# A depthwise convolution on four 64x64 tiles of the TensorE array in place of sixteen 32x32 tiles

## Chip, cores, metric

One core of one Trainium2 chip. The metric is device time in microseconds (us) of one execution; medians of several executions are quoted. Ratios compare fast runs alone: a run more than 1.5% above the fastest of its kernel counts as slow. (Single runs of a one-core program have no state of their own and are marked.)

## The reference

Pooled attention, then a gated feed-forward layer, for 8 batches of 576 tokens. What matters here is the second half, in which the gate is a depthwise convolution of three taps along the tokens:

```python
h = np.maximum(x @ w_in, 0.0)                 # x: 8 x 576 x 512, h: 8 x 576 x 1024
for k in range(3):
    conv_out += conv_w[k] * hp[:, k:k + S, :] # hp: h padded by one token on both sides
gate = 1.0 / (1.0 + np.exp(-conv_out))
return (h * gate) @ w_out
```

## The kernel before

The channels of h lie on the partitions, 8 blocks (`fb`) of 128, tokens along the free dimension. `mm1` makes one block of h, with the relu on ScalarE. `conv` is done by TensorE: three taps, each a product with a diagonal matrix, accumulated in PSUM. A 128x128 diagonal matrix wastes nearly all of the array, so the kernel uses 32x32 tiles: quarter `r` of block `j` goes through the tile in row `r` and column `(r + j) % 4`. All 16 tiles then work at once on four blocks, but block `j` comes out turned by `j` quarters. `gate` multiplies tanh of it with h, partition by partition, so it needs h turned in the same way; SBUF-to-SBUF copies make that turned h. Shortened:

```python
def h_row(b, fb):
    g, j = divmod(fb, NQ)                                  # NQ = 4, QD = 32
    return hT[b % 2][:, g, j + NQ - 1 if j else 0, :]

def mm1(b, fb):                                            # (products into ps cut)
    nc.scalar.activation(out=row..., in_=ps[:, :, 0:SC], func=ACT.Relu, scale=0.5)
    g, j = divmod(fb, NQ)
    if j:
        turned = hT[b % 2][:, g, j, :]
        cut = P - QD * j
        nc.sync.dma_start(out=turned[P - cut:P, PAD:S + PAD], in_=row[0:cut, PAD:S + PAD])
        nc.sync.dma_start(out=turned[0:P - cut, PAD:S + PAD], in_=row[cut:P, PAD:S + PAD])

def conv(b, g, c2):                                        # 4 blocks, half of the tokens
    ps = [slot("c_ps") for _ in range(2)]
    for kk in range(KW):
        for j in range(NQ):
            for r in range(NQ):
                c = (r + j) % NQ
                nc.tensor.matmul(out=ps[j // 2][QD * c:QD * (c + 1), j % 2, 0:SC],
                                 lhsT=dw[QD * r:QD * (r + 1), kk, g * NQ + j, :],
                                 rhs=row[QD * r:QD * (r + 1), o0:o0 + SC], ...)
    for i in range(2):
        nc.scalar.activation(out=tg[:, 2 * i:2 * i + 2, :], in_=ps[i][:, :, 0:SC], func=ACT.Tanh)

def gate(b, g, c2):                                        # VectorE: (tanh + 1) * turned h
    nc.vector.tensor_scalar(out=t1, in0=tg, scalar1=1.0, scalar2=None, op0=OP.add)
    nc.vector.tensor_tensor(out=gT..., in0=t1, in1=hT[b % 2][:, g, 0:NQ, ...], op=OP.mult)
```

PSUM is cut into four slots of two banks, and every product takes the next slot in turn, so TensorE can be held up until ScalarE or VectorE has emptied an old one. The instruction order is fixed by hand: the attention of batch b+1 is woven into the feed-forward layer of batch b.

The softmax here doesn't subtract the row's maximum and nothing guards it: scores larger than these inputs give would overflow.

Of the kernel before, what the change touches and what calls it, by code (L numbers as in the profile page):

```python
# [9 lines left out]
FP32 = mybir.dt.float32  # L10
BF16 = mybir.dt.bfloat16
AX = mybir.AxisListType
OP = mybir.AluOpType
ACT = mybir.ActivationFunctionType

@with_exitstack
def kernel(
# [10 lines left out]
    nc = tc.nc  # L28

    B, H, S, D = q.shape  # L30
# [3 lines left out]
    P = 128  # L34
# [4 lines left out]
    SC = 288  # L39
    NS = S // SC  # L40
# [2 lines left out]
    n_dmc = d_model // P  # L43
    n_fb = d_ff // P
    KW = 3
    QD = 32
    NQ = P // QD
    n_grp = n_fb // NQ
    PAD = 2
    tok0 = [0, 128, 256, 384, S - P]  # L50

    const_pool = ctx.enter_context(tc.tile_pool(name="const", bufs=1))
# [13 lines left out]
    def slot(name):  # L66
        return psum.tile([P, 2, BANK], FP32, name=name, tag="slot")

    def slot16(name):
        return psum.tile([P, 2, 2 * BANK], BF16, name=name, tag="slot")  # L70

    ident = const_pool.tile([P, P], BF16)
# [4 lines left out]
    w_out_sb = const_pool.tile([P, n_fb, d_model], BF16)  # L77
    cw_rows = const_pool.tile([KW * n_fb, P], FP32)
    convw = const_pool.tile([P, KW * n_fb], FP32)
    tile_id = const_pool.tile([P, QD], FP32)  # L80
    dw = const_pool.tile([P, KW, n_fb, QD], BF16)
    kz = [const_pool.tile([P, H, 2, Sp], BF16, name=f"kz{i}") for i in range(2)]
    va = [const_pool.tile([Sp, H, D + 1], BF16, name=f"va{i}") for i in range(2)]
    hT = [
        const_pool.tile([P, n_grp, 2 * NQ - 1, S + 2 * PAD], BF16, name=f"hT{i}") for i in range(2)
    ]

    def h_row(b, fb):
        g, j = divmod(fb, NQ)
        return hT[b % 2][:, g, j + NQ - 1 if j else 0, :]  # L90

    kv_view = "h (sp p) d -> sp h p d"
    q_view = "h (g r) d -> (h g) (r d)"
# [3 lines left out]
    def load_k(b, h0, n):  # L97
        if h0 == 0:
            st[b] = {"k": kv_pool.tile([Sp, H, POOL, D], BF16, name="kr")}
        nc.gpsimd.dma_start(  # L100
            out=st[b]["k"][:, h0:h0 + n], in_=k[b, h0:h0 + n].rearrange(kv_view, p=POOL)
        )
# [8 lines left out]
    def load_q(b):  # L111
        st[b]["q"] = q_pool.tile([P, NI, 2 * D], BF16, name="qr")
        nc.gpsimd.dma_start(  # L113
            out=st[b]["q"].rearrange("p i x -> p (i x)"), in_=q[b].rearrange(q_view, g=QG)
        )

    def landed(ap):
        nc.gpsimd.tensor_copy(out=seen, in_=ap)
# [114 lines left out]
    def mm1(b, fb):  # L233
        xT = st[b]["xT"]
        ps = slot("h_ps")
        for c in range(NS):
            for dc in range(n_dmc):
                nc.tensor.matmul(  # L238
                    out=ps[:, c, 0:SC],
                    lhsT=w_in_sb[:, dc, fb * P:(fb + 1) * P],  # L240
                    rhs=xT[:, dc, c * SC:(c + 1) * SC],
                    start=(dc == 0),
                    stop=(dc == n_dmc - 1),
                )
        row = h_row(b, fb)
        nc.scalar.activation(  # L246
            out=row[:, PAD:S + PAD].rearrange("p (c n) -> p c n", c=NS),
            in_=ps[:, :, 0:SC],
            func=ACT.Relu,
            scale=0.5,  # L250
        )
        g, j = divmod(fb, NQ)
        if j:
            turned = hT[b % 2][:, g, j, :]
            cut = P - QD * j
            nc.sync.dma_start(out=turned[P - cut:P, PAD:S + PAD], in_=row[0:cut, PAD:S + PAD])
            nc.sync.dma_start(out=turned[0:P - cut, PAD:S + PAD], in_=row[cut:P, PAD:S + PAD])

    def conv(b, g, c2):
        if "gT" not in st[b]:  # L260
            st[b]["gT"] = (
                st[b - 1]["gT"] if b % 2 else gT_pool.tile([P, n_fb, 2 * S], BF16, name="gT")
            )
        gT = st[b]["gT"]
        ps = [slot("c_ps") for _ in range(2)]
        for kk in range(KW):
            o0 = PAD - 1 + c2 * SC + kk
            for j in range(NQ):
                row = h_row(b, g * NQ + j)
                for r in range(NQ):  # L270
                    c = (r + j) % NQ
                    nc.tensor.matmul(  # L272
                        out=ps[j // 2][QD * c:QD * (c + 1), j % 2, 0:SC],
                        lhsT=dw[QD * r:QD * (r + 1), kk, g * NQ + j, :],
                        rhs=row[QD * r:QD * (r + 1), o0:o0 + SC],
                        start=(kk == 0),
                        stop=(kk == KW - 1),
                    )
        tg = tg_pool.tile([P, NQ, SC], BF16, name="tg")
        for i in range(2):  # L280
            nc.scalar.activation(  # L281
                out=tg[:, 2 * i:2 * i + 2, :], in_=ps[i][:, :, 0:SC], func=ACT.Tanh
            )
        st[b]["tg", g, c2] = tg

    def gate(b, g, c2):
        tg = st[b].pop(("tg", g, c2))
        t1 = tg_pool.tile([P, NQ, SC], BF16, name="tg1")
        nc.vector.tensor_scalar(out=t1, in0=tg, scalar1=1.0, scalar2=None, op0=OP.add)
        g0 = (b % 2) * S + c2 * SC  # L290
        nc.vector.tensor_tensor(  # L291
            out=st[b]["gT"][:, g * NQ:(g + 1) * NQ, g0:g0 + SC],
            in0=t1,
            in1=hT[b % 2][:, g, 0:NQ, PAD + c2 * SC:PAD + (c2 + 1) * SC],
            op=OP.mult,
        )

# [19 lines left out]
    def load_w_in(i, n):  # L317
        w = d_ff // n
        nc.gpsimd.dma_start(
            out=w_in_sb[:, :, i * w:(i + 1) * w],  # L320
            in_=moe_w_in.rearrange("(c p) f -> p c f", p=P)[:, :, i * w:(i + 1) * w],
        )

    def load_w_out(j):
        src = moe_w_out.rearrange("(g j p) m -> j p g m", j=NQ, p=P)
        dst = w_out_sb.rearrange("p (g j) m -> j p g m", j=NQ)
        cut = P - QD * j
        nc.gpsimd.dma_start(out=dst[j, P - cut:P], in_=src[j, 0:cut])
        if j:
            nc.gpsimd.dma_start(out=dst[j, 0:P - cut], in_=src[j, cut:P])  # L330

    def build_conv_w():
        ps = slot("cw_ps")
        nc.tensor.transpose(
            out=ps[:, 0, 0:KW * n_fb], in_=cw_rows, identity=ident32[0:KW * n_fb, 0:KW * n_fb]
        )
        nc.vector.tensor_copy(out=convw, in_=ps[:, 0, 0:KW * n_fb])
        for r in range(NQ):
            nc.vector.tensor_copy(
                out=tile_id[QD * r:QD * (r + 1), :],  # L340
                in_=ident[QD * r:QD * (r + 1), QD * r:QD * (r + 1)],
            )
        nc.vector.tensor_tensor(
            out=dw.rearrange("p k f j -> p (k f) j"),
            in0=tile_id.unsqueeze(1).to_broadcast([P, KW * n_fb, QD]),
            in1=convw.unsqueeze(2).to_broadcast([P, KW * n_fb, QD]),
            op=OP.mult,
        )

# [8 lines left out]
    def start():  # L358
        nc.sync.dma_start(out=cw_rows, in_=moe_conv_w.rearrange("k (fb p) -> (k fb) p", p=P))
        st[0] = {}  # L360
        load_k(0, 0, HH)
        load_q(0)
        make_identity(nc, ident)
        make_identity(nc, ident32)
        load_k(0, HH, HH)
        for i in range(2):
            nc.vector.memset(kz[i], 0.0)
            nc.vector.memset(va[i][:, :, D], float(POOL))
            nc.gpsimd.memset(hT[i][:, :, :, 0:PAD], 0.0)
            nc.gpsimd.memset(hT[i][:, :, :, S + PAD:S + 2 * PAD], 0.0)  # L370
        landed(st[0]["k"][0:1, 0, 0, 0:1])
        load_v(0, 0, HH)
        landed(st[0]["q"][0:1, 0, 0:1])
        load_v(0, HH, HH)
        landed(st[0]["k"][0:1, HH, 0, 0:1])
        load_w_in(0, 4)
        landed(st[0]["v"][0:1, 0, 0, 0:1])
        load_w_in(1, 4)
        landed(st[0]["v"][0:1, HH, 0, 0:1])
        load_w_in(2, 4)  # L380
        load_w_in(3, 4)
        landed(w_in_sb[0:1, 0, d_ff // 4:d_ff // 4 + 1])
        load_k(1, 0, H)
        landed(w_in_sb[0:1, 0, d_ff - 1:d_ff])
        load_q(1)
        landed(st[1]["k"][0:1, 0, 0, 0:1])
        load_v(1, 0, H)
        landed(st[1]["q"][0:1, 0, 0:1])
        for j in range(NQ):
            load_w_out(j)  # L390
        build_conv_w()
        build_perm()
        k_tree(0, 0, HH)
        k_turn(0, 0, HH)
        q_prep(0, 0, NI // 2)
        q_prep(0, NI // 2, NI // 2)
        for i in range(HH):
            scores(0, i)
        k_tree(0, HH, HH)
        k_turn(0, HH, HH)  # L400
        for i in range(HH, H):
            scores(0, i)
        v_tree(0, 0, HH)
        v_tree(0, HH, HH)
        for i in range(4):
            av(0, i)
        xt(0, [0, 1])
        av(0, 4)
        xt(0, [2, 3])
        xt(0, [4])  # L410
# [175 lines left out]
```

## Time and profile before

| | before |
|---|---|
| median of the first three runs | 250.67 us (248.53 to 253.44) |
| profiled run | 247.42 us, span 245.7 us |
| TensorE, VectorE, ScalarE busy | 89%, 64%, 49% |
| batches 2 to 6, each | 27.06 (even) or 25.67 us (odd) |

The last row is the distance from the first `mm1` product of one batch to that of the next, from the starts of single instructions in the trace. It is the same to 0.02 us in every batch of that kind.

The timeline around the two convolutions that TensorE bounds (start in us, duration, engine, source line, operation, operands, count):

```profile
108.29 0.73 PE L272 MATMUL c_ps<-hT_108,dw 32*32 32x288 bf16 x48
...
108.99 1.19 ACT L281 ACTIVATE tg<-c_ps 128x576 bf16<-128x576 f32 x2
...
110.80 0.73 PE L272 MATMUL c_ps<-hT_108,dw 32*32 32x288 bf16 x48
...
111.50 1.19 ACT L281 ACTIVATE tg<-c_ps 128x576 bf16<-128x576 f32 x2
```

Two tanh of 0.65 us take 1.19 together: each starts before the one ahead of it has ended. The second convolution starts 0.6 us after the tanh of the first have emptied its slots, so it waits for nothing.

### The profile page before, as it was taken

What the parts mean: (1) busy time and instruction counts of PE and PEld (TensorE: products, weight loads), DVE (VectorE), ACT (ScalarE), POOL (GpSimd) and SP (SyncE); (2) the same over time, 40 slices, a digit from 0 to 9 for tenths busy, and PEclk for the clock granted to TensorE, in tenths of its full rate; (3) what the DMA queues carried; (4) which work ended last, traced back from release to release, by engine and by line L of the source; (5) the groups of instructions that cost most, each with busy time, mean ns of one, the idle gap of its engine ahead of it and who ended that gap; (6) DMA issues with size and microseconds to landing.
All of it is one profiled execution on the core that took longest, in us unless ns stands there. A gap on an engine that the chain in (4) does not pass through costs nothing.

```text
span 245.7 us, 7301 instructions
## 1 busy us (share of the span) xinstructions
PE 218.3 (89%) x3153; PEld 142.7 (58%) x3153; DVE 156.9 (64%) x287; ACT 121.3 (49%) x209; POOL 30.9 (13%) x58
## 2 busy tenths in 40 slices
PE   0487998559999999999999999999999999999993
PEld 0455665337666756666566665675666666656441
DVE  5678448683858585668684877668594826553341
ACT  2070379112681659236843586255925693267510
POOL 5442364010200011000200020001000000000000
PEclk9999999756999999999999999999999999999998
DMA  5999899969896288926895589628832223133323
GB/s 82 165 140 135 164 173 219 202 86 142 191 178 153 78 175 128 241 84 120 152 188 137 105 160 186 169 80 177 151 108 69 91 69 95 75 113 95 124 88 128
DMA packets 29908, 33.26 MB, mean 135 GB/s; under 512 B 5788, under 2 KB 24244, under 8 KB 29876
## 3 DMA queue, kind: packets, MB, share of 16 engines
q0 software_dynamic: 16976, 16.27, 45.0%
q1 hardware_dynamic: 12900, 16.54, 20.9%
q8 instruction: 24, 0.39, 0.6%
q14 instruction: 8, 0.07, 0.1%
HBM read 32.52 MB, written 9.44 MB: 171 GB/s over the span
## 4 chain that ended last, share of the span: by engine, by line
PE 62%; ACT 15%; DVE 11%; DMA 5%; issue 5%; POOL 0%; DVEq 0%; SPq 0%; ACTq 0%; POOLq 0%
PE o_ps L304 25%; PE h_ps L238 22%; ACT attnT L181 5%; PE q_ps L160 4%; PE c_ps L272 4%; ACT tg L281 4%; DVE x L205 3%; DVE o L314 3%; DMA qr<-in_q_dram 3%; DMA hT_108<-hT_108 3%; ACT hT_108 L246 3%; ACT hT_109 L246 2%; PE xt_ps L221 2%; PE kT_ps L148 1%; ACT o L312 1%
## 5 line engine op out<-in xcount | busy, mean ns | idle before, releaser
L238 PE MATMUL h_ps<-xT,w_in_sb 128*128 128x288 bf16 x512 | 77.3, 298 | 5.1 <-DVE xT L228 2.3
L304 PE MATMUL o_ps<-w_out_sb,gT 128*128 128x512 bf16 x288 | 67.1, 379 | 0.8 <-DVE gT L291 0.8
L238 PEld LDWEIGHTS <-w_in_sb 128*128 128x128 bf16 x512 | 50.6, 101 | 25.3 <-issue 7.9
L181 ACT ACTIVATE attnT<-sc_ps 72x576 bf16<-72x576 f32 x64 | 37.2, 655 | 19.1 <-PE sc_ps L173 19.1
L304 PEld LDWEIGHTS <-gT 128*128 128x128 bf16 x288 | 27.8, 98 | 29.5 <-DVE gT L291 1.3
L246 ACT ACTIVATE hT_109<-h_ps 128x576 bf16<-128x576 f32 x32 | 21.0, 656 | 44.5 <-PE h_ps L238 44.5
L281 ACT ACTIVATE tg<-c_ps 128x576 bf16<-128x576 f32 x64 | 38.4, 664 | 0.6 <-PE c_ps L272 0.6
L246 ACT ACTIVATE hT_108<-h_ps 128x576 bf16<-128x576 f32 x32 | 21.0, 657 | 24.9 <-PE h_ps L238 24.9
L205 DVE TENSOR_TENSOR x<-av_ps,r 128x512 bf16<-128x512 f32 x40 | 27.7, 692 | 1.4
L314 DVE COPY o<-o_ps 128x512 f32<-128x512 f32 x20 | 13.8, 692 | 18.2 <-PE o_ps L304 18.2
L312 ACT COPY o<-o_ps 128x512 f32<-128x512 f32 x16 | 9.4, 586 | 29.5 <-PE o_ps L304 29.5
L272 PEld LDWEIGHTS <-dw 32*32 32x32 bf16 x1536 | 14.1, 88 | 11.5 <-issue 8.0
L221 PE MATMUL xt_ps<-perm,x 128*128 128x128 bf16 x160 | 15.1, 236 | 5.9 <-DVE x L205 3.9
L221 PEld LDWEIGHTS <-x 128*128 128x128 bf16 x160 | 11.5, 104 | 8.6 <-DVE x L205 7.0
L194 PEld LDWEIGHTS <-attnT 72*128 72x128 bf16 x320 | 13.3, 102 | 4.3 <-ACT attnT L181 0.9
L113 POOL DMA_DIRECT2D qr<-in_q_dram x8 | 4.9, 617 | 81.9 <-PE q_ps L160 79.9
L165 DVE COPY qT<-q_ps 128x1152 bf16<-128x1152 bf16 x16 | 12.1, 756 | 4.8 <-PE q_ps L160 4.5
L173 PE MATMUL sc_ps<-qT,kz_104 128*72 128x288 bf16 x64 | 12.2, 326 | 1.2 <-DVE qT L165 0.8
L160 PE MATMUL q_ps<-ident,qr 128*128 128x128 bf16 x144 | 12.5, 243 | 0.7 <-DMA qr<-in_q_dram 0.7
L204 DVE RECIPROCAL r<-av_ps 128x8 f32<-128x8 f32 x40 | 8.0, 201 | 7.4 <-PE av_ps L194 7.4
L272 PE MATMUL c_ps<-hT_108,dw 32*32 32x288 bf16 x768 | 12.0, 287 | 0.8 <-ACT hT_108 L246 0.5
L228 DVE COPY xT<-xt_ps 128x1024 bf16<-128x1024 bf16 (+1 forms) x24 | 12.0, 548 | 0.1
(163 smaller groups left out, 188.8 us busy)
## 6 DMA issues: line engine op xcount, KB each, us to landing
out_dram<-o SPq DMA_DIRECT2D x36, 256.0 KB, 2.6
qr<-in_q_dram POOLq DMA_DIRECT2D x8, 576.0 KB, 6.2
kr<-in_k_dram POOLq DMA_DIRECT2D x7, 576.0 KB, 11.8
vr<-in_v_dram POOLq DMA_DIRECT2D x7, 576.0 KB, 10.8
hT_108<-hT_108 SPq DMA_DIRECT2D x16, 108.0 KB, 4.6
hT_109<-hT_109 SPq DMA_DIRECT2D x16, 108.0 KB, 4.0
hT_108<-hT_108 SPq DMA_DIRECT2D x16, 72.0 KB, 3.9
hT_109<-hT_109 SPq DMA_DIRECT2D x16, 72.0 KB, 2.2
```

Of the source, the lines that this page charges most:

```text
L160: nc.tensor.transpose(out=ps[:, i * P:(i + 1) * P], in_=st[b]["q"][:, i0 + i, :], identity=ident)
L173: nc.tensor.matmul(out=ps[0:Sp, c2, 0:SC], lhsT=kz[b % 2][:, h, c2, :], rhs=st[b]["qT"][:, h].rearrange("d i g -> d (i g)"), start=True, s ...
L181: nc.scalar.activation(out=at.rearrange("s (i two g) -> s two i g", two=2, g=QG), in_=ps[0:Sp, :, 0:SC].rearrange("s two (i g) -> s two i ...
L194: nc.tensor.matmul(out=ps[:, h // 4, c:c + D + 1], lhsT=st[b]["at"][h][:, t0:t0 + P], rhs=va[b % 2][:, h, :], start=True, stop=True,)
L205: nc.vector.tensor_tensor(out=x.rearrange("p (g h) d -> p g h d", g=2), in0=y[:, :, :, 0:D], in1=r.unsqueeze(3).to_broadcast([P, 2, 4, D]) ...
L221: nc.tensor.transpose(out=y[:, pr, :, ii * RT:(ii + 1) * RT], in_=st[b]["x"][i][:, 2 * pr:2 * pr + 2, :].rearrange("p h d -> p (h d)"), id ...
L238: nc.tensor.matmul(out=ps[:, c, 0:SC], lhsT=w_in_sb[:, dc, fb * P:(fb + 1) * P], rhs=xT[:, dc, c * SC:(c + 1) * SC], start=(dc == 0), stop ...
L246: nc.scalar.activation(out=row[:, PAD:S + PAD].rearrange("p (c n) -> p c n", c=NS), in_=ps[:, :, 0:SC], func=ACT.Relu, scale=0.5,)
L272: nc.tensor.matmul(out=ps[j // 2][QD * c:QD * (c + 1), j % 2, 0:SC], lhsT=dw[QD * r:QD * (r + 1), kk, g * NQ + j, :], rhs=row[QD * r:QD * ...
L281: nc.scalar.activation(out=tg[:, 2 * i:2 * i + 2, :], in_=ps[i][:, :, 0:SC], func=ACT.Tanh)
L304: nc.tensor.matmul(out=ps[:, 0, :], lhsT=gT[:, fb, j * P:(j + 1) * P], rhs=w_out_sb[:, fb, :], start=(fb == 0), stop=(fb == n_fb - 1),)
L314: nc.vector.tensor_copy(out=o, in_=ps[:, 0, :])
```

## The change

With 64x64 tiles there are two halves per block. Two blocks fill the four tiles: one comes out straight, the other with its halves swapped. The intent is to need no turned copy of h at all: tanh reads the swapped halves from PSUM and writes them to the partitions where they belong. This takes one instruction for each half.

```diff
-    const_pool.tile([P, n_grp, 2 * NQ - 1, S + 2 * PAD], BF16, ...)
+    const_pool.tile([P, n_fb, S + 2 * PAD], BF16, ...)
 def mm1(b, fb):
-    (the turned copies: two dma_start for every block with j > 0)
 def conv(b, g, c2):
-        for j in range(NQ):
-            for r in range(NQ):
-                c = (r + j) % NQ
+        for p2 in range(2):
+            for j in range(2):
+                fb = g * NQ + 2 * p2 + j
+                for r in range(2):
+                    c = (r + j) % 2
+                    nc.tensor.matmul(out=ps[j][HP * c:HP * (c + 1), p2, 0:SC],       # HP = 64
+                                     lhsT=dw[HP * r:HP * (r + 1), kk, fb, :],
+                                     rhs=hT[b % 2][HP * r:HP * (r + 1), fb, o0:o0 + SC], ...)
+    pairs = tg.rearrange("p (p2 j) n -> p p2 j n", j=2)
-    for i in range(2):
-        nc.scalar.activation(out=tg[:, 2 * i:2 * i + 2, :], in_=ps[i][:, :, 0:SC], func=ACT.Tanh)
+    nc.scalar.activation(out=pairs[:, :, 0, :], in_=ps[0][:, :, 0:SC], func=ACT.Tanh)
+    for c in range(2):
+        r = 1 - c
+        nc.scalar.activation(out=pairs[HP * r:HP * (r + 1), :, 1, :],
+                             in_=ps[1][HP * c:HP * (c + 1), :, 0:SC], func=ACT.Tanh)
```

Cut: `h_row` is gone, the output weights are loaded straight, in two transfers in place of seven, and the diagonal weights have 64 columns in place of 32.

More of the change, by code (lines that the diff above doesn't have):

```diff
@@ L45 @@
     KW = 3
-    QD = 32
-    NQ = P // QD
-    n_grp = n_fb // NQ
+    HP = P // 2
+    NQ = 4
     PAD = 2
@@ L79 @@
     convw = const_pool.tile([P, KW * n_fb], FP32)
-    tile_id = const_pool.tile([P, QD], FP32)
-    dw = const_pool.tile([P, KW, n_fb, QD], BF16)
+    tile_id = const_pool.tile([P, HP], FP32)
+    dw = const_pool.tile([P, KW, n_fb, HP], BF16)
     kz = [const_pool.tile([P, H, 2, Sp], BF16, name=f"kz{i}") for i in range(2)]
@@ L84 @@
     hT = [
-        const_pool.tile([P, n_grp, 2 * NQ - 1, S + 2 * PAD], BF16, name=f"hT{i}") for i in range(2)
+        const_pool.tile([P, n_fb, S + 2 * PAD], BF16, name=f"hT{i}") for i in range(2)
     ]
-    def h_row(b, fb):
-        g, j = divmod(fb, NQ)
-        return hT[b % 2][:, g, j + NQ - 1 if j else 0, :]
     kv_view = "h (sp p) d -> sp h p d"
@@ L244, in mm1 @@
                 )
-        row = h_row(b, fb)
         nc.scalar.activation(
-            out=row[:, PAD:S + PAD].rearrange("p (c n) -> p c n", c=NS),
+            out=hT[b % 2][:, fb, PAD:S + PAD].rearrange("p (c n) -> p c n", c=NS),
             in_=ps[:, :, 0:SC],
@@ L251, in mm1 @@
         )
-        g, j = divmod(fb, NQ)
-        if j:
-            turned = hT[b % 2][:, g, j, :]
-            cut = P - QD * j
-            nc.sync.dma_start(out=turned[P - cut:P, PAD:S + PAD], in_=row[0:cut, PAD:S + PAD])
-            nc.sync.dma_start(out=turned[0:P - cut, PAD:S + PAD], in_=row[cut:P, PAD:S + PAD])
     def conv(b, g, c2):
@@ L267, in conv @@
             o0 = PAD - 1 + c2 * SC + kk
-            for j in range(NQ):
-                row = h_row(b, g * NQ + j)
-                for r in range(NQ):
-                    c = (r + j) % NQ
-                    nc.tensor.matmul(
-                        out=ps[j // 2][QD * c:QD * (c + 1), j % 2, 0:SC],
-                        lhsT=dw[QD * r:QD * (r + 1), kk, g * NQ + j, :],
-                        rhs=row[QD * r:QD * (r + 1), o0:o0 + SC],
-                        start=(kk == 0),
-                        stop=(kk == KW - 1),
-                    )
+            for p2 in range(2):
[3 more added lines that the diff above has]
+                        c = (r + j) % 2
+                        nc.tensor.matmul(
+                            out=ps[j][HP * c:HP * (c + 1), p2, 0:SC],
+                            lhsT=dw[HP * r:HP * (r + 1), kk, fb, :],
+                            rhs=hT[b % 2][HP * r:HP * (r + 1), fb, o0:o0 + SC],
+                            start=(kk == 0),
+                            stop=(kk == KW - 1),
+                        )
         tg = tg_pool.tile([P, NQ, SC], BF16, name="tg")
-        for i in range(2):
+        pairs = tg.rearrange("p (p2 j) n -> p p2 j n", j=2)
+        nc.scalar.activation(out=pairs[:, :, 0, :], in_=ps[0][:, :, 0:SC], func=ACT.Tanh)
+        for c in range(2):
+            r = 1 - c
             nc.scalar.activation(
-                out=tg[:, 2 * i:2 * i + 2, :], in_=ps[i][:, :, 0:SC], func=ACT.Tanh
+                out=pairs[HP * r:HP * (r + 1), :, 1, :],
+                in_=ps[1][HP * c:HP * (c + 1), :, 0:SC],
+                func=ACT.Tanh,
             )
@@ L293, in gate @@
             in0=t1,
-            in1=hT[b % 2][:, g, 0:NQ, PAD + c2 * SC:PAD + (c2 + 1) * SC],
+            in1=hT[b % 2][:, g * NQ:(g + 1) * NQ, PAD + c2 * SC:PAD + (c2 + 1) * SC],
             op=OP.mult,
@@ L322, in load_w_in, with load_w_out @@
         )
-    def load_w_out(j):
-        src = moe_w_out.rearrange("(g j p) m -> j p g m", j=NQ, p=P)
-        dst = w_out_sb.rearrange("p (g j) m -> j p g m", j=NQ)
-        cut = P - QD * j
-        nc.gpsimd.dma_start(out=dst[j, P - cut:P], in_=src[j, 0:cut])
-        if j:
-            nc.gpsimd.dma_start(out=dst[j, 0:P - cut], in_=src[j, cut:P])
+    def load_w_out(i):
+        n = n_fb // 2
+        nc.gpsimd.dma_start(
+            out=w_out_sb[:, i * n:(i + 1) * n, :],
+            in_=moe_w_out.rearrange("(f p) m -> p f m", p=P)[:, i * n:(i + 1) * n, :],
+        )
     def build_conv_w():
@@ L337, in build_conv_w @@
         nc.vector.tensor_copy(out=convw, in_=ps[:, 0, 0:KW * n_fb])
-        for r in range(NQ):
+        for r in range(2):
             nc.vector.tensor_copy(
-                out=tile_id[QD * r:QD * (r + 1), :],
-                in_=ident[QD * r:QD * (r + 1), QD * r:QD * (r + 1)],
+                out=tile_id[HP * r:HP * (r + 1), :],
+                in_=ident[HP * r:HP * (r + 1), HP * r:HP * (r + 1)],
             )
@@ L344, in build_conv_w @@
             out=dw.rearrange("p k f j -> p (k f) j"),
-            in0=tile_id.unsqueeze(1).to_broadcast([P, KW * n_fb, QD]),
-            in1=convw.unsqueeze(2).to_broadcast([P, KW * n_fb, QD]),
+            in0=tile_id.unsqueeze(1).to_broadcast([P, KW * n_fb, HP]),
+            in1=convw.unsqueeze(2).to_broadcast([P, KW * n_fb, HP]),
             op=OP.mult,
@@ L368, in start @@
             nc.vector.memset(va[i][:, :, D], float(POOL))
-            nc.gpsimd.memset(hT[i][:, :, :, 0:PAD], 0.0)
-            nc.gpsimd.memset(hT[i][:, :, :, S + PAD:S + 2 * PAD], 0.0)
+            nc.gpsimd.memset(hT[i][:, :, 0:PAD], 0.0)
+            nc.gpsimd.memset(hT[i][:, :, S + PAD:S + 2 * PAD], 0.0)
         landed(st[0]["k"][0:1, 0, 0, 0:1])
@@ L388, in start @@
         landed(st[1]["q"][0:1, 0, 0:1])
-        for j in range(NQ):
-            load_w_out(j)
+        for i in range(2):
+            load_w_out(i)
         build_conv_w()
```

## The prediction

> **What bounds the kernel now.** I read the summary page first, then the chain of waits over one steady batch, then the timeline of the same microseconds, then single instructions. The page says that TensorE is nearly full, and that the chain to the end is mostly TensorE's, with ScalarE next:
>
> ```profile
> PE 218.3 (89%) x3153; PEld 142.7 (58%) x3153; DVE 156.9 (64%) x287; ACT 121.3 (49%) x209; POOL 30.9 (13%) x58
> ...
> PE 62%; ACT 15%; DVE 11%; DMA 5%; issue 5%; POOL 0%; DVEq 0%; SPq 0%; ACTq 0%; POOLq 0%
> ...
> L281 ACT ACTIVATE tg<-c_ps 128x576 bf16<-128x576 f32 x64 | 38.4, 664 | 0.6 <-PE c_ps L272 0.6
> ```
>
> ScalarE's 49% is an average over two kinds of stretch. The busy time by stretch (columns: stretch in us, its length, then busy us of PE, PEld, DVE, ACT, POOL, clock, DMA share, GB/s) shows them:
>
> ```profile
> 92.00:98.00 6.00, 5.75 (x139) 3.75 (x137) 3.54 (x7) 5.98 (x12) 0.81 (x1) 1.00 0.83 127
> 106.00:116.00 10.00, 9.95 (x171) 6.57 (x170) 6.78 (x13) 5.10 (x9) 0.59 (x1) 1.00 0.42 96
> ```
>
> In the first, where the convolutions of a batch's first half lie among the last scores, ScalarE has no gap. In the second TensorE has none, and ScalarE is half idle. The chain of waits (start, us, what) agrees: ScalarE's work sets the time until TensorE may start the next first-layer product, because that needs a PSUM slot which a tanh must empty.
>
> ```profile
> 93.56 0.66 ACT hT_108 L246
> 94.22 0.54 ACT tg L281
> 94.75 0.40 issue
> 95.15 0.85 ACT attnT L181 x2
> 96.01 0.21 issue
> 96.22 0.50 ACT hT_108 L246
> 96.72 0.03 issue
> 96.75 0.71 ACT tg L281
> 97.45 0.04 issue
> 97.49 1.14 PE h_ps L238 x8
> ```
>
> Such a stretch comes once in each of batches 1 to 6 (at 67, 92, 119, 145, 172 and 198 us).
>
> The copies of h are hardly on the path. All the waits for them in the list of waits are one line, and both fall in the first batch:
>
> ```profile
> DVE gT L291 <- DMA hT_108<-hT_108: 4.5, 2, 2.6
> ```
>
> **What the Trainium skill says.** "TensorE: Matmul & The Clock Gate", Part 3 (packing small matmuls): products on different tiles of the array start about 4 ns apart and run together, so a packed group lasts about one product. The trace agrees: reading single starts in the convolution at 93.18 us, 16 products start 3.4 ns apart, the next 16 start 134 ns after the first, the last 16 another 185 ns after.
> "TensorEngine Tiling (Array Packing)", Key Properties: changing the tiling mode drains the engine. In the trace the last product of that convolution starts 217 ns before the next full-array one, against 122 ns between two full-array products of the same 288 columns. Both kernels pay this as often.
> "ScalarE: Activation LUTs", What ACT_TABLE_LOAD costs: an ACTIVATE with immediates takes 186 ns + 0.833 ns per element of the free dimension, and back-to-back ones overlap by about 93 ns. For 576 that is 666 ns; measured 664 ns, and 0.53 to 0.54 us from start to start. Partitions don't enter, and the trace's 72-partition exp takes 655 ns. So a tanh on 64 partitions should cost what one on 128 costs.
> "DMA: Bandwidth & Descriptors", Anatomy of one DMA: a fixed cost of about 2 us. The copies land in a median of 2.2 to 4.8 us here, much of it under other work.
>
> **Part by part.**
> *The copies go.* 96 DMA issues leave the SyncE queue and some 7 MB of traffic go. On the path this is worth the one wait in the first batch that nothing else covers: VectorE idle for 1.83 us until 46.07, from where an unbroken VectorE chain leads to the next TensorE work at 51.96. (The other wait, at 37.4, ends inside ScalarE's stretch, which bounds there.) The gate then waits for tanh instead. I move ScalarE's stretch of that batch on by the extra tanh of two convolutions (0.54 us each) less the slack that it has, and the gate starts near 45.15 in place of 46.07: gain 0.9 us.
>
> *The convolution on TensorE.* Per group and half, 48 products in three rounds of 16 become 24 in six rounds of 4. Each streams the same 288 columns, so a round can't be shorter than 288 columns (122 ns in the full-array rows). Now: 134 + 185 + 125 + 222 = 666 ns from its first product to the next mode's first, where 125 is how far the last round's starts are spread and 222 the drain. After: five round steps of 122 to 134 (I take 128), a last round 10 ns wide, and the same drain: 640 + 10 + 222 = 872 ns, or 0.21 us more. I assume that weights are still loaded behind the running round: 48 instructions come together in place of 96, and the 185 ns step of now looks like a queue that has run dry after the first 64. On all 32 convolutions it would be 6.6 us, but where ScalarE bounds most of it is hidden.
>
> *The extra tanh.* The two tanh of a convolution become three, because the two halves of the swapped accumulator go to different partitions: 32 more, at 0.54 us start to start 17.3 us of ScalarE time (21 us in the busy figure, which counts overlaps: 121 to 142). In TensorE's stretches ScalarE's gaps take this up (0.39 to 3.2 us before each relu). In ScalarE's stretch, written on from the timeline at 93 us: first convolution ready 0.04 later; third tanh moves the next exps from 95.15 to 95.75; the relu from 96.22 to 96.81; the second convolution, which needs the slot of the first of those exps, ends by 97.3, no later than ScalarE gets to it; first tanh from 96.75 to 97.35; TensorE resumes at 98.05 in place of 97.49. Its next slot is freed by the third tanh at 99.08, just after TensorE has finished on the first, so the output product starts at 99.12 in place of 98.47. That is 0.65 us, with this stretch's convolutions in it.
>
> *The sum.* Batches 2 to 6: 0.65 in ScalarE's stretch and 2 x 0.21 + 0.03 in TensorE's, 1.1 x 5 = 5.5. Batch 1: 0.65. Batch 7, with no attention beside it: 4 x 0.21 = 0.8. Tail: the gate before the last output products waits for a longer convolution and a third tanh, 0.21 + 0.54, about 0.8. First batch: -0.9. Total 6.85: 250.67 + 6.85 = 257.5 us, 2.7% slower.
>
> *No cost either way*: the gate's VectorE work (760 ns, same shapes), the diagonal weights built once with 64 columns in place of 32 (959 ns, perhaps 1.8, under start-up loads), the output weights in two loads in place of seven.
>
> **The rivals.**
> (1) *Weight loads are not hidden.* A load for a 64-wide tile carries 64 columns, and the trace has no tile of that shape. If every step were the 185 ns of today's third step, a convolution would take 925 + 10 + 222 = 1157 ns, 0.49 us more; with half of that exposed in ScalarE's stretches this adds 6 us to my sum: 263. Against it: the first two rounds now load 32 tiles' weights without delay. I give this 15%.
> (2) *The copies cost more than their waits.* They share the DMA engines with the loads of q, k and v, whose busy share is above 1.0 between 15 and 52 us. If loads land sooner and the first batch tightens further, 2 to 4 us come back. There is also a throttle: from 46.0 to 59.7 us the granted clock is 0.5, after TensorE has idled beside that VectorE chain; a shorter idle might avoid or shorten it, worth up to 4 us. Against: in my count TensorE still idles 5 us there. Result 253 to 255. I give this 25%.
> (3) *ScalarE's stretch has slack that I don't see*, or the scores come early enough to refill it; then only the convolutions on TensorE's stretches remain: 5 x 0.45 + 0.8 + 0.8 - 0.9 = 3, so 253.6. Against: the busy time of 5.98 in 6.00.
>
> **Range and chances.** The rivals give 253 to 263 around 257.5, and before's own three runs spread over 248.5 to 253.4. I take 253.5 to 262. Slower by 2% means above 255.7: 0.68. Within 2%: 0.29. Faster by 2% would need the throttle gone and the extra tanh free: 0.03.
>
> **What would show each step right or wrong.** TensorE: 24 products per convolution, six rounds about 128 ns apart, 0.87 us to the next mode; 0.66 or 1.15 would show that step wrong. ScalarE: 96 tanh at about 660 ns, 64-partition ones no shorter, 142 us busy. The chain through the stretch near 92 us should hold one more tanh in the middle, and a pair of batches, now 27.06 + 25.68 us, should take about 55. No wait for h copies; the gate near 46 us released by ScalarE. A chain that stays with TensorE throughout, or a half-clock stretch that goes, would make the prediction too high; steps of 185 ns or more make it too low.

## The result

The changed kernel takes 258.87 us (257.91 to 259.77, 4 runs) against 250.40 (248.53 to 253.44, 4 runs). Ratios in this text are the mean time of one kernel's fast runs over that of the other's in the same rounds, so they are not quite the ratio of the medians: here 1.036, 95% interval 1.029 to 1.044 (without before's 253.44, which counts as slow). The change is 3.6% slower.

On the page of the changed kernel, the lines that answer to those of before:

```profile
PE 223.3 (87%) x2385; PEld 148.2 (58%) x2385; DVE 158.2 (62%) x285; ACT 147.2 (57%) x241; POOL 28.0 (11%) x53
...
PE 57%; ACT 20%; DVE 12%; DMA 6%; issue 3%; POOL 0%; POOLq 0%
...
L273 ACT ACTIVATE tg<-c_ps 64x576 bf16<-64x576 f32 x64 | 41.3, 645 | 1.2
...
L270 ACT ACTIVATE tg<-c_ps 128x576 bf16<-128x576 f32 x32 | 20.8, 650 | 3.4 <-PE c_ps L261 3.3
```

ScalarE's share of the chain rises from 15% to 20%. A tanh on half the partitions takes as long as one on all (645 and 650 ns). The chain of waits through a ScalarE stretch (here that of batch 3), to be held against the ten lines in the prediction:

```profile
123.80 0.66 ACT hT_109 L240
124.46 0.58 ACT tg L270
125.04 0.03 issue
125.06 0.64 ACT tg L273
125.70 0.01 issue
125.72 0.57 ACT tg L273
126.29 0.10 issue
126.39 1.18 ACT attnT L176 x2
127.57 0.54 ACT hT_109 L240
128.11 0.55 ACT tg L270
128.66 0.04 issue
128.70 1.14 PE h_ps L233 x8
```

From the relu to TensorE's next product it was 3.93 us (93.56 to 97.49; it is 3.93 in batch 3 too, 120.62 to 124.55), now it is 4.90. The first convolution's three tanh stand in the chain, and they no longer overlap: from 124.39 the starts of single instructions are 0.67, 0.65 and 0.67 us apart, where they were 0.53 to 0.55.

And where TensorE bounds:

```profile
110.79 0.93 PE L261 MATMUL c_ps<-hT_108,dw 64*64 64x288 bf16 x24
...
111.76 0.65 ACT L270 ACTIVATE tg<-c_ps 128x576 bf16<-128x576 f32 x1 [0.21 <-PE c_ps L261]
...
112.43 1.30 ACT L273 ACTIVATE tg<-c_ps 64x576 bf16<-64x576 f32 x2
...
113.53 1.18 PE L261 MATMUL c_ps<-hT_108,dw 64*64 64x288 bf16 x24
```

The first convolution of a pair takes 0.87 us to the next product of another kind, as forecast: the starts of its six rounds are 147, 123, 125, 121 and 123 ns apart, and the drain after it is 215. The second takes 1.12. It starts at 113.53, before the third tanh of the first has ended at 113.73; two of its products run, the third waits for ScalarE's semaphore until 113.78, and the others stay a round behind.

### The profile page after: what moved, and what is told of

Its sections match the earlier page's. It is cut to its first block, busy times and chain, and to the rows that moved or that the text cites. A ratio compares the mean times of both kernels' runs of the same rounds, so it can differ in the third digit from the quotient of the medians.

```text
span 257.0 us, 5560 instructions
## 1 busy us (share of the span) xinstructions
PE 223.3 (87%) x2385; PEld 148.2 (58%) x2385; DVE 158.2 (62%) x285; ACT 147.2 (57%) x241; POOL 28.0 (11%) x53
## 4 chain that ended last, share of the span: by engine, by line
PE 57%; ACT 20%; DVE 12%; DMA 6%; issue 3%; POOL 0%; POOLq 0%
PE o_ps L298 24%; PE h_ps L233 18%; ACT attnT L176 6%; PE c_ps L261 6%; DMA qr<-in_q_dram 6%; ACT tg L273 5%; PE q_ps L155 4%; DVE x L200 4%; ACT tg L270 3%; DVE o L308 3%; ACT hT_108 L240 3%; ACT hT_109 L240 2%; PE xt_ps L216 2%; PE sc_ps L168 1%; PE av_ps L189 1%
## 5 line engine op out<-in xcount | busy, mean ns | idle before, releaser
L233 PE MATMUL h_ps<-xT,w_in_sb 128*128 128x288 bf16 x512 | 75.7, 294 | 5.9 <-DVE xT L223 2.5
L273 ACT ACTIVATE tg<-c_ps 64x576 bf16<-64x576 f32 x64 | 41.3, 645 | 1.2
L240 ACT ACTIVATE hT_109<-h_ps 128x576 bf16<-128x576 f32 x32 | 20.8, 651 | 33.2 <-PE h_ps L233 32.9
L261 PEld LDWEIGHTS <-dw 64*64 64x64 bf16 x768 | 22.1, 105 | 13.9 <-issue 12.0
L200 DVE TENSOR_TENSOR x<-av_ps,r 128x512 bf16<-128x512 f32 x40 | 27.7, 692 | 1.4
L270 ACT ACTIVATE tg<-c_ps 128x576 bf16<-128x576 f32 x32 | 20.8, 650 | 3.4 <-PE c_ps L261 3.3
L261 PE MATMUL c_ps<-hT_108,dw 64*64 64x288 bf16 x384 | 16.7, 287 | 2.6 <-ACT attnT L176 1.1
L216 PE MATMUL xt_ps<-perm,x 128*128 128x128 bf16 x160 | 14.0, 227 | 4.8 <-DVE x L200 3.1
L261 PE MATMUL c_ps<-hT_109,dw 64*64 64x288 bf16 x384 | 16.4, 286 | 1.6 <-ACT attnT L176 1.1
L216 PEld LDWEIGHTS <-x 128*128 128x128 bf16 x160 | 10.8, 100 | 7.2 <-DVE x L200 5.9
L189 PEld LDWEIGHTS <-attnT 72*128 72x128 bf16 x320 | 12.1, 99 | 4.5 <-DVE gT L285 1.4
```

The lines of the kernel that those rows point to most:

```text
L189: nc.tensor.matmul(out=ps[:, h // 4, c:c + D + 1], lhsT=st[b]["at"][h][:, t0:t0 + P], rhs=va[b % 2][:, h, :], start=True, stop=True,)
L200: nc.vector.tensor_tensor(out=x.rearrange("p (g h) d -> p g h d", g=2), in0=y[:, :, :, 0:D], in1=r.unsqueeze(3).to_broadcast([P, 2, 4, D]) ...
L216: nc.tensor.transpose(out=y[:, pr, :, ii * RT:(ii + 1) * RT], in_=st[b]["x"][i][:, 2 * pr:2 * pr + 2, :].rearrange("p h d -> p (h d)"), id ...
L233: nc.tensor.matmul(out=ps[:, c, 0:SC], lhsT=w_in_sb[:, dc, fb * P:(fb + 1) * P], rhs=xT[:, dc, c * SC:(c + 1) * SC], start=(dc == 0), stop ...
L240: nc.scalar.activation(out=hT[b % 2][:, fb, PAD:S + PAD].rearrange("p (c n) -> p c n", c=NS), in_=ps[:, :, 0:SC], func=ACT.Relu, scale=0.5,)
L261: nc.tensor.matmul(out=ps[j][HP * c:HP * (c + 1), p2, 0:SC], lhsT=dw[HP * r:HP * (r + 1), kk, fb, :], rhs=hT[b % 2][HP * r:HP * (r + 1), f ...
```

## The experiments

Batch lengths from the traces, in us, mean of an even and an odd batch between 2 and 6, hold most of the answer:

| run | tiles | tanh per convolution | even, odd batch | mean | against before |
|---|---|---|---|---|---|
| before | 32x32, copies | 2 | 27.06, 25.67 | 26.37 | |
| e7 (no transfers for h) | 32x32 | 2 | 27.06, 25.67 | 26.37 | 0.00 |
| e3 | 32x32, copies | 3, in place | 28.05, 26.67 | 27.36 | +1.00 |
| e1 | 64x64 | 2 | 27.59, 26.20 | 26.90 | +0.53 |
| e2 | 64x64 | 3, in place | 28.42, 27.03 | 27.73 | +1.36 |
| e8 | 64x64 | 3, in place, upper half first | 28.56, 27.17 | 27.87 | +1.50 |
| changed | 64x64 | 3, moved | 28.71, 27.32 | 28.02 | +1.65 |
| e5 | 64x64 | 2, moved by VectorE | 27.73, 26.39 | 27.06 | +0.69 |
| e6 | 32x32, copies | 2, one relu on VectorE | 26.84, 25.45 | 26.15 | -0.22 |

e4 and e9 have the lengths of before, e10 those of e6.

Several of these pass the comparison with the reference although tanh lands on the wrong channels. The comparison is not sharp enough to see the gate's small part, so passing it says little about these runs.

### e1: two tanh, halves left swapped

```diff
-        for c in range(2): ... (two 64-partition tanh)
+        nc.scalar.activation(out=pairs[:, :, 1, :], in_=ps[1][:, :, 0:SC], func=ACT.Tanh)
```

> The changed kernel with the swapped accumulator emptied by one 128-partition tanh in place of two 64-partition ones; its result is wrong on purpose (the halves stay swapped). Theory A, most of the loss is the third tanh on ScalarE: what stays is the longer convolution on TensorE (about 0.2 us for each of the 4 of a batch that TensorE bounds) less about 1 us of the first batch, so 252 to 254 us against 250.4 for the kernel before, and the second convolution of each pair falls from 1.12 and 1.53 us to about 0.87. Rival B, the 64x64 tiles are what costs: it stays near 258. The spacing of the two tanh, which still write with the stride of the pairs, is 0.54 us if the stride has nothing to do with the 0.65 us that the changed kernel shows, and 0.65 if it has.

Measured: 250.68 us, below the 252 to 254 expected; ratio to before 1.014 (1.003 to 1.024). The tanh are 0.55 us apart, so the stride of the output is innocent, and each convolution that TensorE bounds takes 0.87 us. Theory A holds: without the third tanh most of the loss is gone. What the tiles cost by themselves is 0.53 us per batch; the moved third tanh is the other 1.12.

### e2: three tanh, each in place

```diff
-            r = 1 - c
+            r = c
```

> The changed kernel with its three tanh, but each 64-partition tanh writes to the partitions that it reads from; wrong on purpose. If moving to other partitions is what keeps consecutive tanh from overlapping (0.65 us from start to start, where two 128-partition tanh took 0.54), the spacing falls to 0.54 and the time to 255.5 to 257 us. If it is the split into halves, the spacing stays at 0.65 and the time within 0.5% of the changed kernel, 258 to 259.5.

Measured: 257.39 us, ratio 1.040 (1.029 to 1.051). Neither expectation was right. From the 128-partition tanh to the lower half the distance is 0.53 to 0.55 us, from the lower to the upper half 0.64 to 0.66, from the upper half to what follows 0.67 to 0.69. So neither moving nor splitting as such prevents the overlap. The in-place third tanh still costs 0.83 us per batch (27.73 against 26.90), moving it 0.29 more.

### e3: the kernel before, with a third tanh

```diff
-        for i in range(2): ... (two 128-partition tanh)
+        nc.scalar.activation(out=tg[:, 0:2, :], in_=ps[0][:, :, 0:SC], func=ACT.Tanh)
+        for c in range(2):
+            nc.scalar.activation(out=tg[64 * c:64 * (c + 1), 2:4, :],
+                                 in_=ps[1][64 * c:64 * (c + 1), :, 0:SC], func=ACT.Tanh)
```

> The kernel before (32x32 tiles, copies kept) with its second tanh split into two 64-partition halves in place; right result. Theory A: it pays the third tanh alone, 0.65 to 1.0 us in each of the six ScalarE stretches and about 1 us in the first batch and the tail, so 255 to 257.5 us. Rival B: no more than 252.

Measured: 258.41 us, ratio 1.046 (1.028 to 1.063), as slow as the changed kernel, with no 64x64 tile in it. 1.00 us per batch is at the upper end of what was expected; the total is above it, because this run's first batch was long too (31.0 us from its first `mm1` to the second batch's, 27.7 in the first profile of before; see e7).

### e8: upper half before lower

```diff
-        for c in range(2):
+        for c in (1, 0):
             r = c
```

> The in-place three tanh, with the upper half (partitions 64 to 127) before the lower; wrong on purpose. If consecutive ScalarE instructions overlap only when they start at the same partition, then 128-partition to upper half takes 0.65 us or more from start to start, upper to lower 0.64, and lower half to the next instruction falls from 0.67 to 0.53. If 64-partition instructions don't overlap with what follows them, the last stays at 0.67 and the first at 0.53.

One look, 259.31 us (state unknown). The distances are 0.67 us from 128 partitions to the upper half, 0.66 from the upper to the lower, 0.55 from the lower half to the next instruction. That is the first expectation. In all pairs seen here, ScalarE instructions overlap when both start at partition 0, whatever their number of partitions (72 to 128 in the same traces: 0.53), and lose 0.10 to 0.16 us where the input or the output of one of them starts at partition 64. In the changed kernel all three steps are of the second kind. No run has two in a row that both start at 64, so whether the change of the start costs this, or the start at 64 itself, stays open. The two-line timeline of each run shows it; in-place order first (e2), reversed order second (e8):

```profile
124.26 0.65 ACT L270 ACTIVATE tg<-c_ps 128x576 bf16<-128x576 f32 x1
124.81 1.29 ACT L273 ACTIVATE tg<-c_ps 64x576 bf16<-64x576 f32 x2
```

```profile
125.56 0.65 ACT L270 ACTIVATE tg<-c_ps 128x576 bf16<-128x576 f32 x1
126.24 1.30 ACT L273 ACTIVATE tg<-c_ps 64x576 bf16<-64x576 f32 x2
```

The second line starts 0.55 us after the first in e2, and 0.68 in e8.

### e4 and e7: the kernel before without its copies

e4 only drops the copies; e7 also loads the output weights as the changed kernel does.

```diff
-        if j: ... (the two dma_start of each turned block)
-    return hT[b % 2][:, g, j + NQ - 1 if j else 0, :]
+    return hT[b % 2][:, g, j, :]
```

> The kernel before without its copies of h: convolution and gate both read the unturned h; wrong on purpose. Theory A: the copies are hidden save for one wait of the first batch, so 249 to 250 us, 0 to 0.6% faster. Rival C, their traffic slows other transfers: 246 to 248 us.

> The kernel before with 32x32 tiles, but without the copies of h and with the output weights loaded in two unturned loads, so that every transfer is as in the changed kernel; wrong on purpose (tanh is applied to the wrong quarter). Theory A, hidden copies: 0 to 0.6% faster than before. Rival C, the copies disturb other transfers: 0.8 to 1.5% faster, and a smaller spread between runs, as the 246.6 to 247.5 against 246.1 to 251.1 of the earlier run without copies hints.

e4: 247.23 us, ratio 0.999 (0.989 to 1.009): inconclusive. (It failed the comparison, since its output weights stayed turned.) e7, with more rounds: 246.41 us, ratio 0.988 (0.983 to 0.993). In batches 2 to 6 the copies cost nothing, to 0.01 us. Yet e7 is 1.2% faster, in the middle of what rival C expected; the smaller spread that it also expected hardly came (2.6 us, 3.0 for before beside it). The gain lies ahead of batch 2: the first batch takes 25.9 us in place of 27.7 in the first profile of before. e7 changes two things, and how much of the gain is the copies' is not separated. e4, which drops the copies alone, has a first batch of 27.3 us; no copy is on its chain there, but the load of k for batch 1, which landed at 29.2 us (28.1 in e7).

### before_again: why the runs of before differ

> The kernel before, profiled a second time, to see where its runs differ. If the copies and the prefetches make the first batch vary: batches 2 to 6 take 27.06 and 25.67 us as in the first profile, and the difference of the whole time lies between 24 and 80 us.

252.89 us (one run, state unknown). As expected, batches 2 to 6 take 27.05 and 25.67 us again; the first takes 32.9 us, and batch 1 0.4 us more. In the first batch the chain of waits holds two long pieces, the load of q for batch 1 and a copy of h; the first profile has the products of `mm1` where this one has the load. First profile of before, then this one:

```profile
24.24 6.37 PE h_ps L238 x32
...
39.19 6.66 DMA hT_108<-hT_108
```

```profile
23.79 9.64 DMA qr<-in_q_dram
...
41.96 9.01 DMA hT<-hT
```

The load landed at 33.4 us, against 30.1, and so the copy starts 2.8 us later; the copy itself takes 2.3 us more. Together this is 5.1 of the 5.2 us by which the first batch is longer. That the whole spread of before, 246.1 to 253.4 us over all its runs, arises there is likely, but just two were profiled. The copy shares the DMA engines with the loads for later batches (their mean busy share is 1.24 from 40 to 45 us in the first profile), and the gate waits for it. Each profile also has a spell at half clock near here: 13.7 us of it in both profiles of before and 17.1 in e3, against 10.2 in e4 and e7 and 6.8 for the changed kernel in this place (e7 and the changed kernel had another 6.8 us some 20 us into the run). What starts it is not shown: in the first profile it begins at 46.0 us, 0.65 us after TensorE fell idle, but in e3 at 46.5, 2.1 us before the idle time of 3.05 us there. In the changed kernel the chain through this batch has no copy, and VectorE's gate there starts at 47.03, against 46.07 and 51.19 in the two profiles of before.

### e5: VectorE moves the halves

```diff
+        (two 128-partition tanh, as in e1)
-        nc.vector.tensor_scalar(out=t1, in0=tg, scalar1=1.0, ...)
+        nc.vector.tensor_scalar(out=dst[:, :, 0, :], in0=src[:, :, 0, :], scalar1=1.0, ...)
+        for c in range(2):
+            r = 1 - c
+            nc.vector.tensor_scalar(out=dst[HP * r:HP * (r + 1), :, 1, :],
+                                    in0=src[HP * c:HP * (c + 1), :, 1, :], scalar1=1.0, ...)
```

> The changed kernel with two 128-partition tanh, and the halves moved back by VectorE: its addition of 1.0 to tanh is split into one instruction for the unswapped blocks and two 64-partition ones for the swapped; right result. Theory A (ScalarE's third tanh is the loss, VectorE has room in the same stretch): as the two-tanh run, 250.5 to 252.5 us, 0.5 to 1.5% above the kernel before. If VectorE's three instructions (estimate: 0.3 us each in place of one of 0.46) come onto the path, 253 to 256.

Measured: 252.96 us, ratio 1.015 (1.008 to 1.022), 0.46 us above the upper end of the first expectation; right result. The three instructions take 0.30 us each, and the batch costs 0.16 us more than e1's (27.06 against 26.90). This is about 6 us less than the changed kernel's median of other rounds, and still slower than before: 0.69 us in each steady batch, against a gain that can lie in the first two batches alone.

### e6, e9 and e10: two small changes to the kernel before

e6 gives VectorE the relu of the fifth `mm1` of a batch and pools the keys ahead of it; e9 lets the third batch's loads of q and v wait in the first batch until the last copy of h has landed; e10 does both.

```diff
+        pool_keys(b + 2)                                    # e6
-        mm1(b, order[4])
+        mm1(b, order[4], on_vector=b + 1 < B)
...
         att[4]()
+        landed(hT[0][0:1, 1, 3, PAD:PAD + 1])               # e9
+        load_q(2)
+        load_v(2, 0, H)
         conv(0, 1, 0)
```

Cut: the VectorE relu itself and the old place of `pool_keys` (e6); the condition that drops the two loads from their old place (e9).

> The kernel before, with one relu of each ScalarE stretch (the fifth of a batch, in batches 1 to 6) done by VectorE, and the pooling of the keys issued ahead of it so that it doesn't block it; right result. If ScalarE bounds that stretch, 0.53 us less of it is worth 0.4 to 0.6 us in each of six batches: 246.5 to 248.5 us against 250.0. If something else ends the stretch, no change, or slower where VectorE becomes late for the gate.

> The kernel before with its copies, but in the first batch the loads of q and v for the third batch wait until the last copies of h of that batch have landed; right result. Rival C as it now stands (the copies cost 1.8 us or more in the first batch alone, because they share the DMA engines with prefetches that could wait): the copy on the chain falls from 6.7 us to about 3, the first batch to 26.0 to 27.0 us (27.7 with the prefetches beside it), 247 to 248.5 us against 249. If the copies are slow by themselves: no change.

> The two small changes together: one relu of each ScalarE stretch on VectorE, and the two loads later; right result. If they add: 0.22 us in each of batches 2 to 6 and the first batch's gain, 245 to 247 us, 1 to 2% faster than the kernel before and 4.5% faster than the changed kernel.

e6: 246.75 us, ratio 0.990 (0.984 to 0.996), 0.22 us per steady batch and not 0.4 to 0.6; six batches of it are 1.3 of the 2.5 us, and the rest is not explained. With 0.53 us less of ScalarE's work the chain through the stretch is TensorE's up to the first convolution, so the rest of the relief falls off the chain:

```profile
121.20 1.08 PE h_ps L238 x8
122.28 0.61 PE c_ps L282 x40
122.89 0.02 issue
122.92 0.73 ACT tg L291 x2
```

e9: 247.32 us, ratio 0.993 (0.986 to 0.999). The copy on the chain still takes 6.06 us, not the 3 expected, and the first batch of the profiled run takes 27.7. But its six runs lie within 246.8 and 248.6, while before ranged over 248.0 to 252.7 beside it. The total is as expected, the two steps to it are not. That the two loads cause the long first batches is supported by this, not proved. e10: 246.27 us, ratio 0.988 (0.981 to 0.996), right result. It has the lowest median of the correct versions, 1.2% ahead of the kernel before, but its runs overlap those of e6.

## Why the prediction was right, and where it was not

The median lies within its range and 1.4 us above its figure, and the mechanism was the one that it gave: ScalarE bounds a stretch of each batch, a third tanh lengthens that, and the copies were hidden in the steady state.

- **Convolution on TensorE.** Forecast 0.872 us, measured 0.866; the weights of a 64x64 tile do load behind the round that runs. Rival 1 is out. The sum came out better than its terms: the steps are 147 and then 121 to 125 ns, not 128, and the drain 215. (The drain after the convolution at 93.18 us is 219 ns, not the 217 that the prediction read.) e1 gives the tiles 0.53 us per batch: 0.43 where TensorE bounds (forecast 0.45), the rest in ScalarE's stretch.
- **Extra tanh, ScalarE's stretch.** Forecast 0.65 us per batch, measured 0.97 (11.43 us, from 113.12 to 124.55 in before; 12.40, from 116.30 to 128.70, after). The term that failed is "at 0.54 us start to start". It took the spacing of two 128-partition tanh for the new ones; with halves that start at partition 64 they are 0.65 to 0.68 apart. The busy figure agrees: 147 us and not 142, as overlaps have gone. Rival 3 is out.
- **Extra tanh, TensorE's stretch.** Forecast 0.45 us per batch, all of it the convolutions', measured 0.68 (97.49 to 113.12 before, 99.99 to 116.30 after). "In TensorE's stretches ScalarE's gaps take this up" failed narrowly: at 0.54 us the third tanh would have freed its slot just in time; at 0.65 it came 0.2 late, and the second convolution of each pair grew by 0.25.
- **Batches 2 to 6 together.** Forecast 5.5 us, measured 5 x 1.65 = 8.2.
- **Batch 1.** Forecast +0.65; 28.10 us after against 28.19 and 28.56 in the two profiles of before. The shorter half-clock spell probably pays for the tanh here (5.5 us of it fall in this batch, 7.7 and 8.5 in the profiles of before); no run tests it.
- **Last batch and tail.** Forecast 0.8 + 0.8, measured 2.2: from batch 7's first product to the end 32.97 us before, 35.19 after.
- **First batch.** Forecast -0.9 net. In the profiles it is 28.05 us after, against 27.72 and 32.91 before. Rival 2 was right in part: without the copies and with the lighter weight loads e7 is 3 us faster by its ratio, all of it before the steady state. The step that failed is "On the path this is worth the one wait": it read one profile, and that was one of the kernel's shorter runs. Two readings under rival 2 were off. The clock falls at 46.0 us, before the VectorE chain of 46.07 begins, so the idle time beside that chain can't be its cause. And the DMA share is not above 1.0 throughout: 0.90 and 0.96 from 25 to 30 and 30 to 35 us.

The errors had opposite signs. 3.3 us too little for tanh, slots and tail was partly made up by about 2 us of gain too little, by difference, in the first two batches; the closeness of 257.5 to 258.87 is partly luck. How much a typical first batch of before costs is known only through the time of the whole run, since just two were profiled.

## What to carry to other kernels

Copies that the chain of waits doesn't contain in the steady state were free there, and what replaces them must be free too. Here 7 MB of hidden traffic was traded for an instruction on the one engine that had no gap in that stretch, though it was idle half of the time on average. Cost an extra instruction in the stretch where it will stand, at the start-to-start distance that instructions of its own form show there, and look for the next PSUM slot that it frees. When runs of one kernel scatter by 3%, compare lengths of equal batches between traces: 0.02 us could be resolved here, and the difference of two profiles of one kernel was found to live in the first two batches.

## What the Trainium skill lacked or had wrong

- "ScalarE: Activation LUTs" has back-to-back ACTIVATEs overlap. It lacks the condition: 0.53 to 0.55 us from start to start where inputs and outputs of both start at partition 0 (a 64-partition tanh after a 128-partition one included), 0.64 to 0.69 where one of them starts at partition 64. The overlap in the first case is 0.10 to 0.12 us, a little more than the page has.
- "TensorE: Matmul & The Clock Gate", Part 3, gives one packed group. For accumulating groups that follow each other the runs show rounds of four 64x64 tiles 121 to 125 ns apart for 288 columns, the first step 147; rounds of sixteen 32x32 tiles 134 and then 185 ns apart. "TensorEngine Tiling (Array Packing)" has the drain without a figure: in batches 2 to 6, 211 to 223 ns from the last product of such a group to the first in another tile mode.
- No page gives the cost of writing to other partitions than those read. It does not show in an instruction's own time: on VectorE 0.30 us for 64 x 576 bf16 elements moved within SBUF with an addition, and 0.30 for 128 x 576 not moved; on ScalarE 0.65 us for either tanh.
